# Where a fused attention and expert kernel loads its small constants, and four moves beside it

## The chip, the cores and the metric

One core of a Trainium2 chip. The time is that of the device in microseconds (us), the median of several executions; lower is better.

## The reference

Float32 throughout. Attention over 4 batches, 8 heads, 768 positions, head size 64, with a window and a linear bias:

```python
scores = scale * np.matmul(q, k.transpose(0, 1, 3, 2))
is_global = pos[None, :] < int(n_global)                  # 8
is_local = (rel >= 0) & (rel < int(n_local))              # 96
dist = np.where(is_global & ~is_local, float(n_local), np.abs(rel))
scores = np.where(is_global | is_local, scores - slopes[:, None, None] * dist, -1e9)
a = softmax(scores)
x = np.matmul(a, v)                                       # rows of 512, 3072 tokens
logits = x @ w_gate + modality_bias[modality_id]          # 8 experts
e_idx = np.argmax(logits, axis=1)
out[mask] = gate_w[mask, None] * (np.maximum(x[mask] @ w1[e], 0.0) @ w2[e])
```

Each token goes to one expert and is scaled by that expert's probability.

## The kernel before, in words

The 3072 tokens are 24 blocks of 128 (`NBLK`), six to a batch. The attention half runs as 25 steps (`step(n)`, lines 1257 to 1322) that work on several blocks at a time: step n computes the scores of block n (`s_mm`, line 209, TensorE, eight heads in the order 7, 0, 2, 3, 4, 5, then 1, 6), adds the bias table and finds each row's extreme (`mx`, line 224, VectorE, one instruction per head), takes exponentials (`ex`, line 240, ScalarE), multiplies block n - 2 with the values (`pv`, lines 279 and 290, TensorE, a part with the small tiles `vl` and one with the large tiles `va`), divides by the row sums (`rinv`, `xr`), transposes the exponentials of block n - 1 (`t_mm`, line 254) and copies them out of PSUM as `pT` (`t_cp`: the first and third copy on ScalarE, the second on VectorE, line 261 or 263). The gate of older blocks (`gate_a` to `gate_d`, lines 335 to 360) runs in the same steps, and after the last block of a batch its routing: `route_a`, `route_a2`, `route_e`, `route_b` (counts by two matmuls at lines 411 and 412, a copy to SBUF at line 414, running sums on GpSimd at line 417), `route_d` and `route_c` (scatter of token numbers, line 440). From batches 0 and 1 the first three expert slots are planned in steps 17 and 18 (`plan_0` to `plan_3`, VectorE), and their weights are loaded and split meanwhile (line 657 on GpSimd, lines 646 and 661 on VectorE). The expert half (two layers in split float32, lines 689 to 691 and 731 to 733) follows the steps; the plan of the remaining slots (`items`, `slots`, `granules`) runs beside its first slots, drawn from `rest()` by `fill`.

Three things set the order. On TensorE, ScalarE, VectorE and GpSimd the order of the steps is the order in which the code calls (`manual_schedule`, lines 1237 to 1240); before the steps, and for VectorE and GpSimd in the expert half, a scheduler may move instructions whose inputs are ready (so line 561, a comparison of two constant tiles in `granules`, runs in the first 5 us). Extra work of a step stands in `todo`, `last_work` and `spaced`; `todo[n]` is called after the exponentials of step n and before its transposes, except `route_b` and `route_e`, which wait until the end of the step (`tail_work`). SyncE issues nearly all loads and stores, in its own scheduled order. Completion semaphores are handed out in turn to the transfers of SyncE and ScalarE together, so an issue can stand until the transfer that used its semaphore before has landed.

PSUM: ring `pR` of three banks (scores, one block fills all three: heads 0, 2, 4; heads 1, 3, 5; heads 6, 7), ring `pP` of three (transposes, counts of batches 0 to 2), ring `pX` of two (values).

The start. GpSimd clears the first columns of `kt` (line 124); SyncE loads queries and keys of blocks 0 and 1 (256 and 272 KB a block) and the values of block 0; ScalarE issues the five small loads of `consts_l` (lines 1025 to 1032: gate weights, modality numbers, modality bias and two scalars spread over 128 partitions); TensorE runs 40 warm-up matmuls (line 134). Meanwhile GpSimd and VectorE build a distance tile (lines 145 to 168), from which come two bias tables of eight heads: `tbl0` for the first block of a batch (line 183, ScalarE) and `tbl` for the others (line 185, GpSimd), in the order `HEADS` = 7, 0, 2, 6, 4, 1, 3, 5. The constants are first read in step 3 (`consts_m`, `consts_b`), step 4 (`gate_b`) and step 7 (`consts_d`).

Of the kernel before, what the change touches and what calls it, by code (L numbers as in the profile page):

```python
# [14 lines left out]
ALU = mybir.AluOpType  # L15
# [6 lines left out]
NP = H // 2  # L22
DM = H * D
E = 8
FF = 1024
NT = B * S
NBLK = NT // P
NG0, NL0 = 8, 96
NB = S // P
W = NL0 + NG0 + 64  # L30
C1 = 40
PER = P + NG0
# [4 lines left out]
BE = 2  # L37
# [5 lines left out]
NR = NI - NS  # L43
NGT = 16
# [13 lines left out]
D1 = D + 1  # L58
HEADS = (7, 0, 2, 6, 4, 1, 3, 5)


def bc(ap, n):
    return ap.unsqueeze(2).broadcast_to([ap.shape[0], ap.shape[1], n])


def bm(ap, n):
    return ap.unsqueeze(1).broadcast_to([ap.shape[0], n, ap.shape[1]])
# [3 lines left out]
def moe_attention_kernel(ctx, tc, q, k, v, qs, ks, vr, vo32, n_global, n_local, modality, w_gate, mod_bias, w1, w2, out):  # L71
    nc = tc.nc
# [7 lines left out]
    def p_p(name):  # L80
        return psum.tile([P, 512], F32, tag="pP", name=name, bufs=3)
# [4 lines left out]
    def p_t(name):  # L86
        return psum.tile([P, 512], F32, tag="pR", name=name, bufs=3)
# [33 lines left out]
                vo32[b, i, h].rearrange("p x a d -> p (x a d)"),  # L121
            )

    nc.gpsimd.memset(kt[:, :, 0:PER], 0.0)
    load_kq(0)
    load_kq(1)
    loadv(0)
# [39 lines left out]

    V.tensor_add(mm0, mm0, dd)

    ident = const.tile([P, P], F32, name="ident")  # L170
    make_identity(nc, ident)
    prs = [a1.tile([P, PRW], F32, name=f"pr{i}") for i in range(NPR)]
# [3 lines left out]

    last = [None]

    def table(t, h, m):

        f = -8.0 * 2.0 ** (-(h + 1))
        if t is tbl0:
            last[0] = nc.scalar.mul(t[:, h, :], m, f)
        else:
            nc.gpsimd.tensor_scalar(t[:, h, :], m, f, None, ALU.mult)  # L185


    blk, pss, scs, pts, gt, lgts, rt, xrs = {}, {}, {}, {}, {}, {}, {}, {}
# [79 lines left out]

    pxs = {}

    def pv(n):
        m = n + 2
        r = n % NV
        px = pxs[n] = [p_x(f"x{n}_{h}") for h in range(2)]
        for hp in range(NP):
            for h in range(2):
                hs = slice(64 * h, 64 * h + C1)
                for half in range(2):
                    nc.tensor.matmul(  # L279
                        px[h][64 * half : 64 * half + 64, hp * D1 : (hp + 1) * D1],  # L280
                        pT_of(n, hp, 1)[hs, 64 * half : 64 * half + 64],
                        vl[r][hs, half, hp, :],
                        start=(hp == 0),
                        stop=False,
                        skip_group_check=True,
                    )
        for hp in range(NP):
            for h in range(2):
                for half in range(2):
                    nc.tensor.matmul(  # L290
                        px[h][64 * half : 64 * half + 64, hp * D1 : (hp + 1) * D1],
                        pT_of(n, hp, 2 * h)[:, 64 * half : 64 * half + 64],
                        va[r][:, half, 2 * hp + h, :],
                        start=False,
                        stop=(hp == NP - 1),
                        skip_group_check=True,
                    )
        if n > 2:
            gate_c(*gates(n - 3), px[1])
        if n > 1:  # L300
            if m in pss:
                gate_b(*gates(n - 2), pss.pop(m)[2], 2 * W)
            else:
                gate_b(*gates(n - 2), p_t(f"lp{m}"), 0)
# [89 lines left out]
    def behind(ins, other):  # L394

        if other is not None:
            tc.add_manual_dep(
                ins.ins,
                other.ins.name,
                mybir.DependencyInfo(mybir.DependencyClass.Sync, mybir.DependencyReason.DATA),  # L400
                reason="spaced",
            )

    def route_b(b, pk=None, o=NP * D1 + 32):


        oh = rt.pop(b)
        if pk is None:
            pk, o = p_t(f"pk{b}"), 0
        ohf = oh.rearrange("p a e -> p (a e)")  # L410
        nc.tensor.matmul(pk[:, o : o + NB * E], tri, ohf, start=True, stop=True)
        nc.tensor.matmul(pk[:, o + NB * E : o + 2 * NB * E], ones, ohf, start=True, stop=True)
        pks = gp.tile([P, 2 * NB * E], F32, tag="pks", name=f"pks{b}", bufs=1)
        V.tensor_copy(pks, pk[:, o : o + 2 * NB * E])
        eng = nc.gpsimd if b + 1 < B else V
        for j in range(NB):
            eng.tensor_add(base[:, b, j + 1, :], base[:, b, j, :], pks[:, (NB + j) * E : (NB + j + 1) * E])
        if b + 1 < B:
            eng.tensor_copy(base[:, b + 1, 0, :], base[:, b, NB, :])
        pos = t3(b, "pos")  # L420
        eng.tensor_tensor(pos, pks[:, 0 : NB * E].rearrange("p (a e) -> p a e", e=E), base[:, b, 0:NB, :], ALU.add)
        eng.tensor_tensor(pos, pos, bm(ebase, NB), ALU.add)
        eng.tensor_tensor(pos, pos, oh, ALU.mult)
        rt[b, "pos"] = pos
# [114 lines left out]
    def granules(uex, ust, uli):  # L539

        def pl(name, shape, dt=F32):
            return plan.tile([P] + shape, dt, name=f"g{name}")

        iex, ist, ili = uex[:, NS:NI], ust[:, NS:NI], uli[:, NS:NI]
        nr = pl("nr", [NR])
        V.tensor_sub(nr, ili, ist)
        h1 = pl("h1", [NR])
        V.tensor_scalar(h1, nr, 0.0, None, ALU.is_gt)  # L550
        h2 = pl("h2", [NR])
        V.tensor_scalar(h2, nr, 128.0, None, ALU.is_gt)
        m = pl("m", [1])
        V.reduce_sum(m, h1, axis=AX.X)
        m2 = pl("m2", [1])
        V.reduce_sum(m2, h2, axis=AX.X)
        gi = uidx[:, 0:NGT]
        gm = pl("gm", [NGT])
        V.tensor_scalar(gm, gi, m, None, ALU.subtract)
        s1 = pl("s1", [NGT, NR])  # L560
        V.tensor_tensor(s1, bc(gi, NR), bm(uidx[:, 0:NR], NGT), ALU.is_equal)
        V.tensor_tensor(s1, s1, bm(h1, NGT), ALU.mult)
        s2 = pl("s2", [NGT, NR])
        V.tensor_tensor(s2, bc(gm, NR), bm(uidx[:, 0:NR], NGT), ALU.is_equal)
        V.tensor_tensor(s2, s2, bm(h2, NGT), ALU.mult)
        yield
        gst, gex, gli = pl("st", [NGT]), pl("ex", [NGT]), pl("li", [NGT])
        w = pl("w", [NGT, NR])
        wr = pl("wr", [NGT])
        V.reduce_sum(wr, s2, axis=AX.X)  # L570
        V.tensor_add(s1, s1, s2)
        for dst, src in ((gst, ist), (gex, iex), (gli, ili)):
            V.tensor_tensor(w, s1, bm(src, NGT), ALU.mult)
            V.reduce_sum(dst, w, axis=AX.X)
        V.scalar_tensor_tensor(gst, wr, 128.0, gst, ALU.mult, ALU.add)
        V.tensor_add(m, m, m2)
        V.tensor_sub(m2, gli[:, NGF:NGR], gst[:, NGF:NGR])
        V.tensor_scalar(m2, m2, float(MR), None, ALU.is_gt)
        V.scalar_tensor_tensor(m2, m, float(NGR), m2, ALU.is_gt, ALU.max)
        V.tensor_scalar(m, m, -float(NGF), 0.0, ALU.add, ALU.max)  # L580
        V.tensor_mul(m, m, m2)
        V.tensor_copy(lcnt, m)

        V.tensor_scalar(m, m, 1.0, None, ALU.min)
        V.tensor_copy(m2, flag)
        V.tensor_tensor(m, m, m2, ALU.max)
        V.tensor_copy(past, m)
        yield
        return gex, gst, gli
# [392 lines left out]
    def at(n, f, *args):  # L982
        todo.setdefault(n, []).append((f, args))
# [92 lines left out]
        nc.gpsimd.memset(lto, 0)  # L1076
        nc.gpsimd.memset(ltv, 0.0)

    consts_l()

    nid = (E * NT + U) * IDW // P
    zrow = a2.tile([P, nid // 8], I32, name="zrow")

# [9 lines left out]
    for b in range(B):  # L1093
        n0 = b * NB
        at(n0 + NB + 4, route_a, b)
        at(n0 + NB + 4, route_a2, b)
        at(n0 + NB + 4, route_e, b)
        at(n0 + NB + 4, route_b, b)
        if b != BE:
            at(n0 + NB + 5, route_d, b)  # L1100
        for j in range(NB):
            if b < BE:
                spaced.setdefault(n0 + NB + 5 + (j if j < 4 or not b else j - 1), []).append((b, j))
            else:
                at(max(n0 + NB + 5, NBLK + 1), route_c, b, j)
    at(1, consts_a)
    at(3, consts_m)
    last_work[3] = [(consts_b, ())]
    for j in range(8):
        at(3 + j, consts_c, j)  # L1110
    at(7, consts_d)
    for h in HEADS:
        table(tbl, h, mm)
    load_kq(2)

# [141 lines left out]
    def step(n):  # L1257
# [2 lines left out]
        load(n)  # L1260
        work, mid_work, tail_work = todo.pop(n, []), [], []
        if on:
            s_mm(n, (7, 0, 2, 3, 4, 5))
            mx(n, 7)
            s_mm(n, (1, 6))
            for hh in HEADS[1:]:
                mx(n, hh)
            if n == 1:
                t_mm(0, 0)
                t_cp(0, 0, True)  # L1270
            for hh in HEADS:
                ex(n, hh)
                if hh == 0:
                    mark[0] = last[0]
        if n > 1:
            pv(n - 2)
        if len(spaced.get(n, ())) > 1:
            route_c(*spaced[n].pop(0), mark[0])
# [31 lines left out]
        if n > 2:  # L1310
            gate_a(*gates(n - 3))
        for f, args in tail_work:
            if f is route_b:
                args += (p_p(f"pk{args[0]}"), 0)
            f(*args)
        for f, args in last_work.pop(n, []):
            if f in (split, ld_w):
# [268 lines left out]
```

## Time and profile before

| | us |
|---|---|
| median of 3 executions | 459.52 (456.77 to 464.5) |
| the profiled execution | 453.91 |
| its span, first to last instruction | 452.2 |
| TensorE busy in it | 432.7 |
| VectorE, ScalarE, GpSimd busy | 301.1, 273.9, 109.3 |

The span is what the views below divide; some 1.7 us of the execution lie outside it. The 25 steps of the attention take the first 150 us, 5.44 us for a step in which nothing waits; the experts take the rest. TensorE's busy time hides two things: matmuls overlap and their ends are modelled, and a matmul at the lower clock counts as busy as one at the higher. A wait for several semaphores is put down to the one that came last by the profile; where the engine named had long been done, it was another, often a transfer.

### The profile page before, as it was taken

The numbers are of one execution on the slowest core, as the hardware profiler recorded it, in microseconds if no ns is written. First come the engines' busy times: TensorE is split into PE (matmuls) and PEld (weight loads), VectorE is DVE, ScalarE is ACT, GpSimd is POOL, SyncE is SP. The second block draws the span as 40 slices with busy tenths as digits, with TensorE's granted clock in tenths as the row PEclk, the third lists the DMA queues.
The fourth block names the chain that finished last, engine by engine and source line by source line (L and its number), as shares of the span: only waits on it lengthen the run. The fifth ranks groups of instructions, "written<-read, shape, count | busy, mean of one in ns | idle before, by whom it ended". The sixth has DMA issues, their size and how long they took to land.

```text
span 452.2 us, 12800 instructions
## 1 busy us (share of the span) xinstructions
PE 432.7 (96%) x4873; PEld 382.1 (85%) x4873; DVE 301.1 (67%) x943; ACT 273.9 (61%) x508; POOL 109.3 (24%) x176
## 2 busy tenths in 40 slices
PE   6999999999989999999999999999999999999990
PEld 5889888887978898989898988989889898989850
DVE  4787888788788768987475696574956746464500
ACT  4788888887876455555464576455864645554420
POOL 8010003122415166330504032121123030301010
PEclk9999999999999999999999999999999999999996
DMA  6999999897958749484858489766797666565500
GB/s 187 328 327 347 345 334 310 248 296 237 290 173 313 247 146 378 161 300 156 308 181 287 162 287 335 233 235 213 250 361 260 224 232 215 181 208 208 188 32 28
DMA packets 58666, 110.24 MB, mean 244 GB/s; under 512 B 9019, under 2 KB 22867, under 8 KB 58596
## 3 DMA queue, kind: packets, MB, share of 16 engines
q1 hardware_dynamic: 53312, 96.39, 63.7%
q0 software_dynamic: 4672, 12.85, 7.6%
q8 instruction: 40, 0.66, 0.6%
q14 instruction: 30, 0.25, 0.2%
q10 hardware_dynamic: 612, 0.10, 0.1%
HBM read 94.95 MB, written 14.43 MB: 242 GB/s over the span
## 4 chain that ended last, share of the span: by engine, by line
PE 74%; issue 13%; DVE 4%; POOL 3%; DMA 2%; ACT 1%; POOLq 0%; SPq 0%; ACTq 0%; DVEq 0%
PE s L209 7%; PE pt L254 6%; PE phs L691 5%; PE phs L689 5%; PE phs L690 5%; PE x L290 5%; PE pos L733 4%; PE pos L732 4%; PE pos L731 4%; PE x L279 3%; PE phe L689 3%; PE phe L691 3%; PE phe L690 3%; PE poe L733 2%; PE poe L732 2%
## 5 line engine op out<-in xcount | busy, mean ns | idle before, releaser
L240 ACT ACTIVATE pr<-sc,nmx 128x168 f32<-128x168 f32 x192 | 67.6, 424 | 14.3 <-DVE nmx L224 11.8
L691 PE MATMUL phs<-xhs,als 128*128 128x256 f32 x256 | 72.4, 283 | 0.0
L689 PE MATMUL phs<-xhs,ahs 128*128 128x256 f32 x256 | 72.4, 283 | 0.0
L690 PE MATMUL phs<-xls,ahs 128*128 128x256 f32 x256 | 72.3, 282 | 0.0
L224 DVE CUSTOM_DVE_ANT_0 sc<-s,tbl 128x168 f32<-128x168 f32 x192 | 52.7, 329 | 20.8 <-PE s L209 20.4
L696 DVE SCALAR_TENSOR_TENSOR hls<-phs,hhs 128x512 fp32r<-128x512 f32 x32 | 22.1, 692 | 51.0 <-ACT hhs L695 51.0
L731 PE MATMUL pos<-bhs,hhs 128*128 128x512 f32 x128 | 52.0, 406 | 0.0
L733 PE MATMUL pos<-bhs,hls 128*128 128x512 f32 x128 | 50.7, 396 | 0.0
L732 PE MATMUL pos<-bls,hhs 128*128 128x512 f32 x128 | 50.5, 395 | 0.0
L613 POOL DMA_INDIRECT xgs<-x_rows,uis x16 | 21.1, 1319 | 118.4 <-DMA uis<-ids_sorted 56.5
L689 PEld LDWEIGHTS phs<-xhs,ahs 128*128 128x128 f32 x256 | 49.0, 191 | 0.4
L690 PEld LDWEIGHTS phs<-xls,ahs 128*128 128x128 f32 x256 | 48.9, 191 | 0.3
L691 PEld LDWEIGHTS phs<-xhs,als 128*128 128x128 f32 x256 | 48.9, 191 | 0.0
L695 ACT ACTIVATE hhs<-phs 128x512 fp32r<-128x512 f32 x32 | 19.1, 597 | 49.1 <-PE phs L691 49.1
L209 PE MATMUL s<-kt,qt 64*64 64x168 f32 x768 | 40.8, 329 | 3.8 <-POOL tbl L185 2.5
L209 PEld LDWEIGHTS s<-kt,qt 64*64 64x64 f32 x768 | 31.8, 141 | 9.1 <-DVE nmx L224 2.7
L254 PE MATMUL pt<-ident,pr 128*128 128x128 f32 x288 | 38.0, 283 | 0.0
L254 PEld LDWEIGHTS pt<-ident,pr 128*128 128x128 f32 x288 | 32.2, 144 | 4.8 <-issue 3.4
L440 POOL DMA_INDIRECT ids_sorted<-tki,pi x24 | 25.8, 1074 | 42.3 <-ACT pr L240 28.9
L261 ACT COPY pT<-pt 128x512 f32<-128x512 f32 x49 | 28.3, 585 | 10.0 <-PE pt L254 9.3
L801 POOL DMA_INDIRECT out<-obs,ois x16 | 17.1, 1067 | 54.9 <-ACT obs L800 52.7
L731 PEld LDWEIGHTS pos<-bhs,hhs 128*128 128x128 f32 x128 | 24.1, 189 | 6.6 <-issue 2.1
(348 smaller groups left out, 1000.1 us busy)
## 6 DMA issues: line engine op xcount, KB each, us to landing
va<-in_vr SPq DMA_DIRECT2D x24, 520.0 KB
kt<-in_ks SPq DMA_DIRECT2D x24, 272.0 KB
qt<-in_qs SPq DMA_DIRECT2D x24, 256.0 KB
x_rows<-xr SPq DMA_DIRECT2D x24, 256.0 KB
vl<-in_vo SPq DMA_DIRECT2D x48, 81.2 KB
rawe0a<-in_moe_w SPq DMA_DIRECT2D x4, 512.0 KB
rawe0b<-in_moe_w SPq DMA_DIRECT2D x4, 512.0 KB
rawe1a<-in_moe_w SPq DMA_DIRECT2D x4, 512.0 KB
```

What stands on the lines that cost most here:

```text
L209: nc.tensor.matmul(ps[g][64 * half : 64 * half + 64, c0 : c0 + W], qt[hs, hp, 64 * half : 64 * half + 64], kt[hs, hp, w0 : w0 + W], start= ...
L224: V.tensor_tensor_reduce(out=sc, in0=pss[n][g][:, c0 : c0 + W], in1=(tbl0 if n % NB == 0 else tbl)[:, hh, :], op0=ALU.add, op1=ALU.min, sc ...
L240: last[0] = nc.scalar.activation(pr[:, h * (PRW - W) : h * (PRW - W) + W], scs.pop((n, hh)), AF.Exp, bias=blk[n][:, hh : hh + 1], scale=-1.0,)
L254: nc.tensor.transpose(tp[:, j * P : (j + 1) * P], prs[(NP * n + hp) % NPR][:, o : o + P], ident)
L261: last[0] = nc.scalar.copy(pT.rearrange("p a b -> p (a b)"), tp)
L440: ins = nc.gpsimd.indirect_dma_start(out=ids, out_offset=bass.IndirectOffsetOnAxis(ap=pi[:, j : j + 1], axis=0), in_=tki[:, b * NB + j, :] ...
L689: nc.tensor.matmul(o, hi[:, fs], s.xh[:, c, :], start=(c == 0), stop=False)
L690: nc.tensor.matmul(o, hi[:, fs], s.xl[:, c, :], start=False, stop=False)
L691: nc.tensor.matmul(o, lo[:, fs], s.xh[:, c, :], start=False, stop=(c == 3))
L731: nc.tensor.matmul(s.po[t], s.hh[:, fc, tt], hi[:, wv], start=(fc == 0), stop=False)
L732: nc.tensor.matmul(s.po[t], s.hh[:, fc, tt], lo[:, wv], start=False, stop=False)
L733: nc.tensor.matmul(s.po[t], s.hl[:, fc, tt], hi[:, wv], start=False, stop=(fc == 7))
```

## The change

1. The memset of `kt` is called after the distance chain, not first on GpSimd.
2. `consts_l` is no longer called ahead of the steps but in step 1's `todo`, behind `consts_a`; its five issues stay on ScalarE, now behind step 1's exponentials and ahead of its third `pT` copy.
3. Of the eight `tbl` tables GpSimd computes five (7, 0, 2, 6, 4); VectorE computes the last three (1, 3, 5) in step 0, behind its eight reductions.
4. In steps 17 and 18 the scores of heads 1 and 6 stand between the two parts of the values of block n - 2 (`mid`), and reductions and exponentials go 7, 0, 2, 4, 3, 6, 1, 5. What followed the values' matmuls in `pv` is now `pv_g`, called behind the exponentials as before.
5. `route_b` of batch 2 leaves the end of step 22: its two matmuls (`route_p`) stand behind the first six heads' scores of step 23, the rest behind that step's reductions. The counts of batch 3, in the expert half, take a bank of `pP`, not of `pR`.
6. The comparison of line 561 gets a wait for the ScalarE instruction called last before it, so it can't run in the first microseconds any more.

```diff
-    nc.gpsimd.memset(kt[:, :, 0:PER], 0.0)
     load_kq(0)
...
     V.tensor_add(mm0, mm0, dd)
+    nc.gpsimd.memset(kt[:, :, 0:PER], 0.0)
     ident = const.tile([P, P], F32, name="ident")
...
-    def table(t, h, m):
+    def table(t, h, m, eng=None):
...
-            nc.gpsimd.tensor_scalar(t[:, h, :], m, f, None, ALU.mult)
+            (eng or nc.gpsimd).tensor_scalar(t[:, h, :], m, f, None, ALU.mult)
...
-    def pv(n):
-        m = n + 2
+    def pv(n, mid=None):
...
+        if mid is not None:
+            mid()
         for hp in range(NP):
...
+        if mid is None:
+            pv_g(n)
+
+    def pv_g(n):
+        m = n + 2
+        px = pxs[n]
         if n > 2:
             gate_c(*gates(n - 3), px[1])
...
+    def route_p(b):
+        o = 0
+        pk = rt[b, "pk"] = p_p(f"pk{b}")
+        ohf = rt[b].rearrange("p a e -> p (a e)")
         nc.tensor.matmul(pk[:, o : o + NB * E], tri, ohf, start=True, stop=True)
         nc.tensor.matmul(pk[:, o + NB * E : o + 2 * NB * E], ones, ohf, start=True, stop=True)
+
+    def route_b(b):
+        oh = rt.pop(b)
+        if (b, "pk") not in rt:
+            rt[b] = oh
+            route_p(b)
+            rt.pop(b)
+        pk, o = rt.pop((b, "pk")), 0
         pks = gp.tile([P, 2 * NB * E], F32, tag="pks", name=f"pks{b}", bufs=1)
...
-        V.tensor_tensor(s1, bc(gi, NR), bm(uidx[:, 0:NR], NGT), ALU.is_equal)
+        behind(V.tensor_tensor(s1, bc(gi, NR), bm(uidx[:, 0:NR], NGT), ALU.is_equal), last[0])
...
-    consts_l()
...
-        at(n0 + NB + 4, route_b, b)
+        if b != BE:
+            at(n0 + NB + 4, route_b, b)
...
     at(1, consts_a)
+    at(1, consts_l)
...
-    for h in HEADS:
+    for h in HEADS[0:5]:
         table(tbl, h, mm)
...
+            split_pv = n in (LAST - 1, LAST)
+            heads = (7, 0, 2, 4, 3, 6, 1, 5) if split_pv else HEADS
             s_mm(n, (7, 0, 2, 3, 4, 5))
+            if n == NBLK - 1:
+                route_p(BE)
             mx(n, 7)
-            s_mm(n, (1, 6))
-            for hh in HEADS[1:]:
+            if split_pv:
+                pv(n - 2, lambda: s_mm(n, (1, 6)))
+            else:
+                s_mm(n, (1, 6))
+            for hh in heads[1:]:
                 mx(n, hh)
+            if n == 0:
+                for h in HEADS[5:]:
+                    table(tbl, h, mm, V)
+            if n == NBLK - 1:
+                route_b(BE)
...
-            for hh in HEADS:
+            for hh in heads:
                 ex(n, hh)
...
-        if n > 1:
+        if on and split_pv:
+            pv_g(n - 2)
+        elif n > 1:
             pv(n - 2)
...
         for f, args in tail_work:
-            if f is route_b:
-                args += (p_p(f"pk{args[0]}"), 0)
             f(*args)
```

## Rows read from the trace of the kernel before

**Rows 1.** The page: busy time, share of the span and instructions of each engine.

```profile
PE 432.7 (96%) x4873; PEld 382.1 (85%) x4873; DVE 301.1 (67%) x943; ACT 273.9 (61%) x508; POOL 109.3 (24%) x176
```

**Rows 2.** Waits of PE, whole span: who waited for whom; us in total, times, longest.

```profile
PE s L209 <- POOL tbl L185: 2.5, 1, 2.5
...
PE s L209 <- DVE nmx L224: 1.4, 3, 0.6
...
PE x L290 <- DMA rawe0a<-in_moe_w: 1.3, 1, 1.3
...
PE pk L411 <- ACT pT L261: 0.6, 3, 0.2
```

**Rows 3.** Timeline, first 12.5 us: start, length, engine, line, operation, count, [idle before].

```profile
0.81 0.55 POOL L124 MEMSET kt<- 128x544 f32 x1 [0.29 <-POOLq L1543]
...
0.81 0.41 ACTq L1025 DMA_DIRECT2D wg<-in_wg  x1
...
1.25 0.65 ACTq L1027 DMA_DIRECT2D mi<-in_moe_modality_id  x1
...
1.93 0.37 ACTq L1029 DMA_DIRECT2D mb<-in_moe_modality_bias  x1
...
2.33 0.45 ACTq L1032 DMA_DIRECT2D gi<-in_n_global  x1
...
2.94 0.26 DVE L154 TENSOR_SCALAR mm<-dd 128x168 f32<-128x168 f32 x1
...
3.63 0.34 ACTq L1032 DMA_DIRECT2D gi<-in_n_local  x1
...
4.38 0.29 DVE L561 TENSOR_TENSOR gs<-uidx 128x144 f32<-128x144 f32 x1
...
5.86 5.26 POOL L185 TENSOR_SCALAR tbl<-mm 128x168 f32<-128x168 f32 x8
...
10.10 0.33 DVE L224 CUSTOM_DVE_ANT_0 sc<-s,tbl 128x168 f32<-128x168 f32 x1 [0.80 <-PE s L209]
...
11.68 0.33 DVE L224 CUSTOM_DVE_ANT_0 sc<-s,tbl 128x168 f32<-128x168 f32 x1
```

**Rows 4.** By stretch: us, busy us of PE, PEld, DVE, ACT, POOL, PEclk, DMA share, GB/s.

```profile
4.00:8.00 4.00, 1.53 (x18) 1.29 (x16) 1.85 (x10) 3.25 (x9) 2.98 (x7) 1.00 0.53 147
...
8.00:16.00 8.00, 7.44 (x74) 6.31 (x75) 4.60 (x33) 3.73 (x11) 3.04 (x5) 1.00 0.98 317
```

**Rows 5.** Waits of SP's own queue, 0 to 9 us.

```profile
SPq L119 <- DMA kt<-in_ks: 3.7, 1, 3.7
```

**Rows 6.** Timeline of PE, 7 to 22 us.

```profile
7.98 2.52 PE L209 MATMUL s<-kt,qt 64*64 64x168 f32 x32 [2.47 <-POOL tbl L185]
...
13.95 2.82 PE L254 MATMUL pt<-ident,pr 128*128 128x128 f32 x12
...
20.18 1.53 PE L254 MATMUL pt<-ident,pr 128*128 128x128 f32 x12
...
21.64 1.56 PE L209 MATMUL s<-kt,qt 64*64 64x168 f32 x32
```

**Rows 7.** Timeline of ACT, 15 to 19 us (step 1 and its copy).

```profile
15.10 0.59 ACT L261 COPY pT<-pt 128x512 f32<-128x512 f32 x1 [2.24 <-PE pt L254]
...
15.58 2.71 ACT L240 ACTIVATE pr<-sc,nmx 128x168 f32<-128x168 f32 x8
...
18.20 0.56 ACT L261 COPY pT<-pt 128x512 f32<-128x512 f32 x1
```

**Rows 8.** Timelines of DVE and PE, step 18.

```profile
106.07 0.68 DVE L263 COPY pT<-pt 128x512 f32<-128x512 f32 x1
...
106.67 0.32 DVE L224 CUSTOM_DVE_ANT_0 sc<-s,tbl 128x168 f32<-128x168 f32 x1
...
107.06 0.36 PE L209 MATMUL s<-kt,qt 64*64 64x168 f32 x2 [0.64 <-DVE nmx L224]
```

**Rows 9.** Timeline of DVE, step 24.

```profile
147.28 1.29 DVE L676 TENSOR_TENSOR xle<-mte,xhe 128x512 fp32r<-128x512 f32 x2
```

More of the change, by code (lines that the diff above doesn't have):

```diff
@@ L402, in behind @@
             )
[L404 to L410, printed above, removed]
+    def route_p(b):
+        o = 0
+        pk = rt[b, "pk"] = p_p(f"pk{b}")
+        ohf = rt[b].rearrange("p a e -> p (a e)")
         nc.tensor.matmul(pk[:, o : o + NB * E], tri, ohf, start=True, stop=True)
         nc.tensor.matmul(pk[:, o + NB * E : o + 2 * NB * E], ones, ohf, start=True, stop=True)
+    def route_b(b):
[5 more added lines that the diff above has]
+        pk, o = rt.pop((b, "pk")), 0
         pks = gp.tile([P, 2 * NB * E], F32, tag="pks", name=f"pks{b}", bufs=1)
```

## The prediction, made before the changed kernel was built or timed

> **What bounds the kernel now.** I read the page first: TensorE is busy for 432.7 of 452.2 us [rows 1], so whatever the change does, it can win back part of some 19 us of idle TensorE and no more. I then asked for the waits of TensorE [rows 2], to see where that idle time lies next to the edits. The largest wait is 2.5 us in front of the first scores (line 209). 1.4 us more come from the same line waiting for VectorE's score reductions (line 224) in three places, and 0.6 us from three waits in front of the routing counts (line 411). The 1.3 us at line 290 names a transfer that the change doesn't touch. So the change has some 4 us within its reach, nearly all in the first 20 us, and I read those closely: the timeline of the start [rows 3], transfers by stretch [rows 4], SyncE's queue [rows 5], TensorE and ScalarE in steps 0 and 1 [rows 6, 7].
>
> The view blames table work on GpSimd for the first wait. That can't be it: what the scores need from GpSimd is the memset of kt, over at 1.36 us [rows 3]. SyncE's queue shows the other candidate: the first vl issue waits 3.7 us for a kt load [rows 5], up to about the moment at which the scores start, 7.98 [rows 6]. So the first keys land at about 7.9 us. In that time the transfer engines are only 0.53 busy and move 147 GB/s, against 317 GB/s just after [rows 4]; the five small constant loads are in flight then [rows 3]. And the matmuls run at the lower of TensorE's two levels (1.2 GHz, not 2.4) through steps 0 and 1, judged by their length: twelve transposes take 2.82 us at 13.95 and 1.53 us at 20.18, 32 score matmuls 2.52 us at 7.98 and 1.56 us at 21.64 [rows 6]. The granted-clock column reads 1.00 in both stretches [rows 4], so here I go by the lengths.
>
> **The change part by part.** I sum against the profiled execution: span 452.2 us, 453.9 in all, 5.6 us below the median of the runs, 459.5.
>
> *Constants out of the start, and the memset behind the table chain.* Queries and keys of block 0 are 528 KB; at 317 GB/s [rows 4] they take 1.7 us, and without the constants I expect them to have landed before the warm-up ends at 5.51 (7.98 minus the idle 2.47 [rows 6]). Scores then start at 5.55, 2.4 us sooner. GpSimd's memset moves by 0.55 us behind the iotas and is still long over. The table chain begins 0.55 us sooner and loses the 0.29 us of the granule comparison (line 561) that VectorE runs inside it [rows 3], so the first table is ready for the first reduction.
>
> *Steps 0 and 1.* VectorE's second score reduction starts 2.12 us after the scores (10.10 against 7.98), and the last 1.58 us after that, with 0.33 us of its own [rows 3]. At the low level that gives 5.55 + 2.12 + 1.58 + 0.33 = 9.6 us. The second half of the next block's scores must wait for this bank: 20 of 32 matmuls, 1.6 us, then four transposes, 0.94 us [rows 6]: 12.2 us, where ScalarE's first pT copy started at 15.10 [rows 7], a gain of 2.9. If TensorE, now busy without a break from the warm-up on, has reached the high level by then, the 2.12 shrink to 1.3 (by 1.56 to 2.52 [rows 6]) and the last reduction ends at 8.8. Then VectorE's three tables, 0.26 us each by the nearest row [rows 3], and the next block's first reduction, for which head 6 waits, come last, 9.9 us, and with head 6 and four transposes (0.1 and 0.5) it is 10.5, a gain of 4.6. I take the middle, 3.7. At the low level the tables' 0.8 us end before the scores do and cost nothing; GpSimd is relieved of 2.0 of its 5.26 us [rows 3].
>
> *What ScalarE pays in step 1.* The five issues now stand on ScalarE between the exponentials of step 1 and ScalarE's second pT copy (block 0's third), which follow each other without a gap (15.58 plus 2.71, next at 18.20 [rows 7]). Behind them wait that copy, hence the second half of block 0's values on TensorE, and all of step 2's exponentials. The issues took 0.41, 0.65, 0.37, 0.45 and 0.34 us [rows 3], 2.2 in sum. Bounds: below, nothing, if ScalarE's sequencer issues them while exponentials still run; above, 2.2 plus a wait. The fifth issue stood 0.85 us behind the fourth's end [rows 3], and SyncE once waited 3.7 us [rows 5] for an earlier transfer: an issue can wait for a landing, and from 8 us on the transfer engines are 0.98 busy [rows 4]. I take 2.2 without a wait, nearest to the five rows. Net for the start: 3.7 - 2.2 = 1.5 us, between 4.6 and 2.9 - 5.9 = -3.0. The constants are first read in steps 3 and 4, some 5 us later. SyncE, no longer behind the constants, issues its loads earlier; those had room already.
>
> *Heads 1 and 6 between the values' parts, steps 17 and 18.* In step 18 TensorE waits 0.64 us for the first score reduction (107.06 [rows 8]). The values' first part would fill that, but it needs the pT copy that VectorE runs from 106.07 to 106.75, right in front of the reduction (106.67 to 106.99) [rows 8]. So TensorE restarts some 0.25 us sooner only, and heads 1 and 6 come some 0.6 us later to a VectorE that is behind. I count 0, between +0.6 (the stall gone) and -0.3 (VectorE later, step 19 waits).
>
> *Batch 2's counts after the first scores of step 23.* TensorE no longer stands in front of them: 0.6 us over three places, 0.2 for this one [rows 2]. VectorE's copy and GpSimd's sums come later in the step, and with them a cast whose remainder VectorE takes ahead of line 676, which ends at 148.57 [rows 9] and feeds the first layer; I count +0.2, between 0 and +0.4 with that in the way.
>
> *Last granule counts behind ScalarE.* One comparison of 0.29 us [rows 3] goes into the expert stage, where TensorE has work without a gap; it would cost 0.3 if VectorE had become late there. 0. Batch 3's counts take a buffer of another ring, at no cost for the same reason.
>
> Sum: 1.5 + 0 + 0.2 + 0 = 1.7 us: 452.2 for a profiled execution, 457.8 us against the median.
>
> **The rivals.**
> *The issues wait on ScalarE (slower).* If the five constants are queued behind transfers that land late, ScalarE stands still with the copy and step 2's exponentials behind it. The start's gain, 3.7 in the middle, is used up when the five take over about 3.7 us together; with one wait of 3.7 the start loses 3.0, with the 0.2 of step 23 in all -2.8: 462.3 us. For it: a transfer engine share of 0.98 [rows 4] and the two waits seen. Against: SyncE issues in the same stretch keep up with TensorE.
>
> *Nothing of the issues is seen, and the clock is high early (faster).* 4.6 + 0.2 = 4.8 us: 454.7. For it: TensorE has no break between warm-up and scores. Against: ScalarE had no gap there [rows 7]. The Trainium skill, page Perfetto Trace Analysis, section Sequencer Loop, has a sequencer push engine work into a queue and go on to the next instruction, which would put the issues beside the exponentials; no run here shows it yet.
>
> *The first keys land no sooner (the change doesn't do what it says).* The constants are 98 KB, 0.3 us at 317 GB/s [rows 4]. If bytes alone count, the scores start 0.3 us sooner, and ScalarE still pays 2.2: 0.3 - 2.2 + 0.2 = -1.7, 461.2 us. The Trainium skill, DMA: Bandwidth & Descriptors, section Issuing engines are not separate DMA queues, speaks for it: issuing from several engines saves only the sequencer's time, as all transfers share the same sixteen engines. Against it the trace has these engines half idle, 0.53, just while the small packets are under way [rows 4].
>
> **How the numbers follow.** Forecast 0.47 (457.8 us), waiting issues 0.20 (462.3), everything hidden 0.20 (454.7), keys no sooner 0.13 (461.2). The three runs before spread over 7.7 us (456.8 to 464.5), more than any of these cases, so the range takes the cases and some of that spread: 452 to 463.5 us. About 2% (9 us) is what a measurement of this kernel can tell from no change, and every case lies within it; only the spread reaches beyond: faster 0.04, same 0.93, slower 0.03.
>
> **What would show it.** Right: the first scores start near 5.5 us with no wait in front; the warm-up and line 209 join; the five issues stand on ScalarE's queue after step 1's exponentials, about 2.2 us long, and the second pT copy follows them at about 17 us; step 2's values wait for that copy; step 3 starts 1 to 2 us before 21.64. The wait at line 411 is gone in step 23 and line 561 has left the start. Wrong: a first score start above 7 us; a gap of several us among the five issues; a longer wait of TensorE in step 2 than the 2.5 us won; a new wait in step 19.

## The result: slower, and the profile after

The changed kernel takes 462.6 us (median of 6 executions, 461.12 to 464.06), the kernel before beside it 456.86 us (6 executions): a ratio of 1.0128 [1.0092, 1.0165], slower by 1.3% or 5.7 us. A second comparison, with an experiment below, gave 1.0169 [1.0132, 1.0206]. Both are under the 2% that the prediction took for what can be told from no change, but neither interval takes in 1. The first three of the six executions before are those of the median of 459.52 us named above; one of them, 464.5 us, fell in a slower state of the chip and is left out of the ratio.

The waits of TensorE in the changed kernel's profile (span 460.8 us, 462.75 us in all) come first, as in [rows 2]. The line numbers have shifted: the values' two parts are lines 278 and 291, the counts lines 416 and 417.

```profile
PE x L278 <- ACT pT L261: 9.3, 1, 9.3
PE x L278 <- issue: 1.9, 3, 1.3
...
PE s L209 <- DMA kt<-in_ks: 0.6, 1, 0.6
...
PE pk L416 <- ACT pT L261: 0.4, 2, 0.2
```

The 2.5 us in front of the first scores [rows 2] have become 0.6, and one of the three waits for the counts is gone. In their place stands one wait of 9.3 us for ScalarE's copy. What ScalarE did then is in its timeline (start, length, engine, line, operation, count, idle before), to be set against [rows 7]:

```profile
11.41 0.59 ACT L261 COPY pT<-pt 128x512 f32<-128x512 f32 x1 [1.09 <-PE pt L254]
11.89 2.71 ACT L240 ACTIVATE pr<-sc,nmx 128x168 f32<-128x168 f32 x8
16.55 0.38 ACTq L1039 DMA_DIRECT2D wg<-in_wg  x1
19.46 0.56 ACTq L1041 DMA_DIRECT2D mi<-in_moe_modality_id  x1
20.43 0.36 ACTq L1043 DMA_DIRECT2D mb<-in_moe_modality_bias  x1
21.82 0.33 ACTq L1046 DMA_DIRECT2D gi<-in_n_global  x1
22.57 0.34 ACTq L1046 DMA_DIRECT2D gi<-in_n_local  x1
22.95 0.59 ACT L261 COPY pT<-pt 128x512 f32<-128x512 f32 x1 [8.34 <-DMA mb<-in_moe_modality_bias]
```

In [rows 7] the second copy follows the eight exponentials without a gap; here 8.35 us lie between (14.60 to 22.95). The five issues are 0.33 to 0.56 us long, 1.97 us together. The rest, 6.4 us, is the time in which ScalarE stands in front of them: 1.95, 2.53, 0.41, 1.03 and 0.42 us. Each of these issues carries a wait on the completion semaphore that it takes over. `wg`'s is that of the queries' load issued at 10.50 us, eight transfers earlier in the order in which semaphores are handed out, and the last `gi` waits for `wg` itself. In the trace these earlier transfers land at 16.53, 19.44, 20.40, 21.80 and 22.55 us, and each issue starts 0.02 to 0.03 us later. For `mb` the chain of work shows it (start, length, what): a load of values from its issue to its landing at 20.40, and 0.02 us behind that the start of `mb`.

```profile
13.42 6.99 DMA vl<-in_vo
20.40 0.02 issue
20.43 2.50 DMA mb<-in_moe_modality_bias
```

The transfer engines are full in this stretch or nearly so, as the view by stretch shows (us, busy us of PE, PEld, DVE, ACT, POOL, granted clock, transfer engines' share, GB/s):

```profile
8.00:16.00 8.00, 5.84 (x100) 4.77 (x100) 7.00 (x48) 5.51 (x17) 1.49 (x3) 1.00 1.10 325
16.00:24.00 8.00, 0.42 (x8) 0.30 (x8) 0.00 (x0) 1.05 (x3) 0.00 (x0) 0.55 0.86 270
24.00:32.00 8.00, 8.00 (x153) 7.56 (x150) 5.04 (x29) 6.20 (x18) 0.00 (x0) 0.81 0.73 234
```

From 16 to 24 us nearly the whole core stands, and TensorE's granted clock falls to 0.55 and is still at 0.81 in the next stretch. TensorE's timeline shows what that costs, beside [rows 6]:

```profile
6.06 1.79 PE L209 MATMUL s<-kt,qt 64*64 64x168 f32 x32 [0.55 <-DMA kt<-in_ks]
...
10.72 1.53 PE L254 MATMUL pt<-ident,pr 128*128 128x128 f32 x12
...
23.58 0.49 PE L278 MATMUL x<-vl,pT 40*64 40x65 f32 x8 [9.30 <-ACT pT L261]
24.01 2.00 PE L291 MATMUL x<-va,pT 128*64 128x65 f32 x32
25.94 2.06 PE L254 MATMUL pt<-ident,pr 128*128 128x128 f32 x12
27.93 1.42 PE L209 MATMUL s<-kt,qt 64*64 64x168 f32 x30
```

The twelve transposes take 1.53 us at 10.72, where [rows 6] have 2.82 for the first block's: before the wait TensorE ran at the higher level (2.4 GHz) already. Behind it the same twelve take 2.06 us. Step 3 starts at 27.93 us, in [rows 6] at 21.64: 6.3 us later, though step 2 started 4.5 us sooner (12.18 against 16.70). From step 3 on the two kernels keep this distance within 0.6 us to step 19. So the loss is in the first 28 us. (The two spans differ by more, 8.6 us; the profiled execution of the kernel before is shorter than its median, 453.91 us, and what lies behind step 19 differs between two profiles of one kernel as well, as shown below.)

### The profile page after: what moved, and what is told of

The parts are those of the page before. It is cut to its first block, busy times and chain, and to the rows that moved or that the text cites. A ratio compares the mean times of both kernels' runs of the same rounds, so it can differ in the third digit from the quotient of the medians.

```text
span 460.8 us, 12810 instructions
## 1 busy us (share of the span) xinstructions
PE 434.0 (94%) x4873; PEld 381.1 (83%) x4873; DVE 301.3 (65%) x946; ACT 274.4 (60%) x508; POOL 109.8 (24%) x173
## 4 chain that ended last, share of the span: by engine, by line
PE 72%; issue 13%; DMA 5%; DVE 4%; POOL 2%; ACT 2%; SPq 0%; POOLq 0%; ACTq 0%; DVEq 0%
PE s L209 6%; PE pt L254 6%; PE phs L705 5%; PE x L291 5%; PE phs L703 5%; PE phs L704 5%; PE pos L747 4%; PE pos L746 4%; PE pos L745 4%; PE x L278 3%; PE phe L703 3%; PE phe L704 3%; PE phe L705 3%; PE poe L747 2%; PE poe L745 2%
## 5 line engine op out<-in xcount | busy, mean ns | idle before, releaser
L209 PE MATMUL s<-kt,qt 64*64 64x168 f32 x768 | 39.2, 314 | 1.3 <-DVE nmx L224 0.6
L454 POOL DMA_INDIRECT ids_sorted<-tki,pi x24 | 26.8, 1117 | 42.1 <-ACT pr L240 32.6
L209 PEld LDWEIGHTS s<-kt,qt 64*64 64x64 f32 x768 | 29.8, 133 | 6.3 <-DVE nmx L224 2.0
L278 PE MATMUL x<-vl,pT 40*64 40x65 f32 x768 | 21.5, 223 | 11.6 <-ACT pT L261 9.3
L815 POOL DMA_INDIRECT out<-obs,ois x16 | 17.6, 1098 | 52.7 <-ACT obs L814 50.6
```

What stands on the lines that cost most here:

```text
L209: nc.tensor.matmul(ps[g][64 * half : 64 * half + 64, c0 : c0 + W], qt[hs, hp, 64 * half : 64 * half + 64], kt[hs, hp, w0 : w0 + W], start= ...
L278: nc.tensor.matmul(px[h][64 * half : 64 * half + 64, hp * D1 : (hp + 1) * D1], pT_of(n, hp, 1)[hs, 64 * half : 64 * half + 64], vl[r][hs, ...
```

## The experiments

**Four ways to place the five loads.** Theory A: the loss is ScalarE's wait for the semaphores of earlier transfers, with the lower clock behind it. First, `consts_l` goes back ahead of the steps and all other edits stay:

```diff
+    consts_l()
...
     at(1, consts_a)
-    at(1, consts_l)
```

> The kernel after, with the five constant loads back ahead of the steps; the other five edits stay. Theory A (the five issues on ScalarE in step 1 each stand until an earlier transfer has landed, and everything behind them waits): the 9.3 us wait of TensorE in step 2 is gone, the scores start at 7 to 8 us again, step 3 starts between 20.3 and 21.6 us, and the time is within 1.5 us of the kernel before, rather below it. Rival B (the other edits cost the time, the issues only show in the trace): still 4 us or more above the kernel before.

Second, the opposite: in the kernel before, `consts_l` alone is moved to step 1, and nothing else.

```diff
-    consts_l()
...
     at(1, consts_a)
+    at(1, consts_l)
```

> The kernel before, with nothing changed but the place of the five constant loads (step 1 on ScalarE). Theory A: ScalarE has a gap of 6 to 9 us between step 1's exponentials and the pT copy, TensorE waits about as long in step 2, step 3 starts 5 to 8 us later than 21.64, and the time is 4 to 8 us above the kernel before. Rival B: no such gap, time within 1.5 us of the kernel before.

Third, GpSimd issues the five in step 1, all other edits stay:

```diff
-        nc.scalar.dma_start(wg.rearrange("p c e -> p (c e)"), w_gate)
+        nc.gpsimd.dma_start(wg.rearrange("p c e -> p (c e)"), w_gate)
...
```

> The kernel after, with the five constant loads issued by GpSimd in the same place of step 1, a queue with completion semaphores of its own. Theory A: ScalarE goes from step 1's exponentials to the copy without a gap, the scores start at about 6 us as in the kernel after, step 3 starts near 17.5 to 18.5 us and the time is 2.5 to 5 us below the kernel before. Rival C (the small transfers themselves, in the full queue, hold up the loads that step 2 needs, whoever issues them): step 3 starts after 21.6 and the time is not below the kernel before.

Fourth, they stay on ScalarE in step 1, but behind the copy and not ahead of it:

```diff
-    at(1, consts_l)
+    last_work[1] = [(consts_l, ())]
```

> The kernel after, with the five constant loads still on ScalarE but at the end of step 1, behind block 0's third pT copy. Theory A: the values of block 0 no longer wait, but the gap of ScalarE stays (5 to 9 us), now ahead of step 2's exponentials; TensorE waits in front of step 2's transposes or step 3 instead, step 3 starts 2 to 6 us after 21.64, and the time is 1 to 6 us above the kernel before. Rival D (only that one copy was in a bad place): step 3 starts at 17.5 to 19 us and the time is 2 us or more below the kernel before.

| loads | ratio to before | step 3 starts at, us | ScalarE's gap in steps 1 and 2 |
|---|---|---|---|
| first: at the start, other edits stay | 0.9983 [0.9944, 1.0023] | 20.21 | none |
| second: ScalarE in step 1, nothing else | 1.0213 [1.0152, 1.0275] | 29.27 | 10.11 |
| third: GpSimd in step 1 | 0.9989 [0.9957, 1.0021] | 17.16 | none |
| fourth: ScalarE, behind the copy | 1.0158 [1.0102, 1.0215] | 17.65, step 4 at 32.08 (27.40 before) | 8.50 |

The move of the loads alone makes the loss, and undoing it alone takes the loss away. Behind the copy the same wait only hits the next thing in ScalarE's queue, the exponentials of step 2; TensorE then waits 5.1 us in the middle of step 3 for the reductions behind them. Some sizes that Theory A gave were missed: the second's gap is longer than 9 us and its median 8.8 us above that of the kernel before, where 4 to 8 was expected, and in the fourth not step 3 comes late but what follows inside it. From GpSimd, whose transfers got semaphores of their own (five that no transfer before had used), the issues wait for nothing:

```profile
9.61 0.79 POOL L1039 DMA_DIRECT2D wg<-in_wg  x1
10.42 0.59 POOL L1041 DMA_DIRECT2D mi<-in_moe_modality_id  x1
10.99 0.55 POOL L1043 DMA_DIRECT2D mb<-in_moe_modality_bias  x1
11.53 0.54 POOL L1046 DMA_DIRECT2D gi<-in_n_global  x1
12.06 0.53 POOL L1046 DMA_DIRECT2D gi<-in_n_local  x1
```

The Trainium skill, DMA: Bandwidth & Descriptors, section Anatomy of one DMA — SWDGE (gpsimd) path, says that DMA engines do not wait on semaphores and that any such wait happens on the issuing sequencer. ScalarE's rows agree: the wait stands in its own queue, ahead of its copy.

The time of the third was a miss: step 3 starts 4.5 us sooner than before, the time is only some 0.5 us lower, and the interval takes in a ratio of 1. Runs further on ask where that lead goes.

**One issue alone.** `wg` stays on ScalarE in step 1, the other four go ahead of the steps.

```diff
-    def consts_l():
+    def consts_w():
         nc.scalar.dma_start(wg.rearrange("p c e -> p (c e)"), w_gate)
+
+    def consts_l():
...
+    consts_l()
...
-    at(1, consts_l)
+    at(1, consts_w)
```

> Only the first of the five loads (wg) stays on ScalarE in step 1, the other four go back ahead of the steps. Theory A: the one issue stands until the queries' load issued eight transfers earlier has landed, at 15 to 17 us, some 1 to 3 us behind step 1's exponentials instead of 8.3 us; ScalarE's next copy follows within 1 us of it, step 3 starts at 20 to 23 us (27.93 with all five), and the time is 455 to 459 us, within 2 us of the kernel before. Rival B (each issue costs ScalarE some 1.7 us of its own in this stretch, 8.3 divided by 5, whatever landed): the gap is 1.7 us, and the issue starts right behind the last exponential, within 0.3 us.

Measured: 459.95 us, 0.9997 [0.9960, 1.0033] of the kernel before (459.67 on this chip), step 3 at 19.85. ScalarE's timeline:

```profile
13.68 2.71 ACT L240 ACTIVATE pr<-sc,nmx 128x168 f32<-128x168 f32 x8
16.01 0.33 ACTq L1039 DMA_DIRECT2D wg<-in_wg  x1
16.39 0.59 ACT L261 COPY pT<-pt 128x512 f32<-128x512 f32 x1
```

Neither theory had this quite right. The issue came at 16.01 as Theory A had it, 0.02 us behind the landing that it waited for (a load of values issued at 10.30, not the queries' load expected), but with four loads at the start the exponentials ran until 16.39, so it stood beside them and the copy followed without a gap. Rival B, a cost of 1.7 us for each issue, falls: an issue whose semaphore comes before the work ahead of it has ended costs ScalarE nothing here. The Trainium skill, Perfetto Trace Analysis, section Sequencer Loop, has the sequencer hand work to its engine and go on; this row agrees, and the changed kernel's rows show its limit: an instruction that waits holds everything behind it.

**SyncE issues the five in step 1**, every other edit stays (`nc.sync.dma_start`).

> The five loads issued by SyncE in step 1, every other edit stays. Theory A: they stand in SyncE's queue for earlier landings as they did on ScalarE, but there only loads are behind them, which have room: ScalarE's copy follows step 1's exponentials within 1 us, step 3 starts at 17 to 19 us, no wait of TensorE in steps 2 to 5 is over 1 us, and the time is within 1 us of that with GpSimd's issues (455 to 457 us). Rival D (the loads behind them come late): a wait of TensorE for keys or values of 2 us or more in steps 2 to 5, step 3 or 4 starts some 2 to 6 us later than with GpSimd's issues, and the time is 459 to 463 us.

```profile
14.83 0.35 SPq L1039 DMA_DIRECT2D wg<-in_wg  x1
15.23 0.84 SPq L1041 DMA_DIRECT2D mi<-in_moe_modality_id  x1
16.11 0.35 SPq L1043 DMA_DIRECT2D mb<-in_moe_modality_bias  x1
16.51 0.43 SPq L1046 DMA_DIRECT2D gi<-in_n_global  x1
17.08 1.45 SPq L1046 DMA_DIRECT2D gi<-in_n_local  x1
```

457.12 us against 459.67, a ratio of 0.9940 [0.9907, 0.9974]; step 3 at 17.62, no wait of TensorE over 0.8 us in steps 2 to 5. The issues come some 5 us later than GpSimd's did: they stand behind SyncE's earlier loads, and the first and the last of them start 0.02 us after a landing that they wait for (14.81 and 17.06). But behind them stand only loads with room. Run again beside GpSimd's on one chip:

> The constants by SyncE in step 1, once more, beside GpSimd's on the same chip: the first gave 0.9940 [0.9907, 0.9974] of the kernel before and the second 0.9989 [0.9957, 1.0021], measured on different chips. Theory A (on either queue ScalarE is free, so the two are the same kernel to TensorE): both lie at 0.991 to 0.998 and within 0.4% of each other. Rival E (GpSimd's issues cost something that SyncE's don't): this one stays at 0.994 or below and GpSimd's at 0.998 or above again.

> The constants by GpSimd in step 1, once more, beside SyncE's on the same chip. Theory A: within 0.4% of SyncE's, 0.991 to 0.998 of the kernel before. Rival E: 0.998 or above, and over 0.4% above SyncE's.

0.9937 [0.9907, 0.9967] by SyncE (449.92 us against 453.16) and 0.9959 [0.9933, 0.9986] by GpSimd, as Theory A had it; the second half of Rival E, 0.998 or above for GpSimd, did not come. SyncE's has the lowest ratio measured, though its interval overlaps that of GpSimd's: it is below the kernel before on two chips, where the changed kernel is above it in both of its comparisons.

**Start edits alone, with GpSimd's issues.** The split in steps 17 and 18 and the move of batch 2's counts are taken back (`split_pv = False`; `route_b` at the end of step 22 again). And the kernel before was profiled once more.

> Theory A (the five issues on ScalarE wait for the landing of earlier transfers whose completion semaphores they take over; nothing else of the change costs more than 0.7 us): with the constants issued by GpSimd in step 1 and the two late edits (heads 1 and 6 in steps 17 and 18, batch 2's counts) taken back, step 3 starts at 17 to 18.5 us as with GpSimd's issues before, steps 17 to 19 take 17.7 to 18.4 us together (18.4 to 18.5 with the split), and step 22 takes 5.8 to 6.0 us (5.43 with the counts moved). In all 2.5 to 4.5 us below the kernel before, 453 to 455. Rival C (the lead won at the start is lost again before the end, in stalls and waits that come wherever the engines run ahead): the time is within 1.5 us of the kernel before, as with GpSimd's issues and all other edits, although step 3 starts 4 us sooner.

> The kernel before, profiled once more, to see how far one profiled execution differs from another in the later stages. Theory A: step 3 starts at 20.5 to 22.5 us again; steps 4 to 16 take 5.2 to 6.2 us each as before; where a stall of 1 to 2 us without a late releaser sits (step 22 in the first profile) differs, so that the stages behind step 16 differ by up to 3 us between the two profiles of the same kernel. Rival C: the later stages agree within 0.5 us, and the differences of 1 to 2.5 us that the changed kernels show behind step 16 are theirs.

The first: 458.87 us against 459.67, 0.9967 [0.9928, 1.0005], step 3 at 17.12. That is 1.5 us below before, not 2.5 to 4.5, and the interval takes in a ratio of 1; so with or without the late edits the time gains less than step 3 does. One place where the lead shrinks is step 12. TensorE's timeline of the kernel with SyncE's issues, in its first run:

```profile
70.90 1.53 PE L254 MATMUL pt<-ident,pr 128*128 128x128 f32 x12
74.02 0.66 PE L342 MATMUL tx<-ident,xr 128*128 128x128 f32 x4 [1.59 <-ACT pT L261]
```

and the same step in its second run:

```profile
70.38 1.53 PE L254 MATMUL pt<-ident,pr 128*128 128x128 f32 x12
71.76 0.66 PE L342 MATMUL tx<-ident,xr 128*128 128x128 f32 x4
```

One kernel, two executions, and step 12 took 7.17 and 5.44 us. This stall of 1.6 to 1.9 us also stood in the profiles of GpSimd's issues (first run), of the start edits alone and of the second experiment, not in either profile of the kernel before. But that kernel loses time in the next step instead: its step 13 takes 5.99 and 6.63 us, that of SyncE's issues 5.72. Over both steps the loss on the chip that profiled both is 0.8 us (12.89 against 12.07). The row at 74.02 blames ScalarE, but ScalarE's own next instruction was waiting for TensorE. The cause of the stall stays open. The second profile of the kernel before (459.51 us) starts step 3 at 21.08 and agrees with the first in steps 3 to 12 within 0.01 us each, yet reaches the first layer of the later expert slots 4.2 us later than the first profile (226.78 against 222.62), more than either expectation had (up to 3 us, and 0.5). So what happens behind step 16 can't be told from one profile of each kernel. It seems to go by the chip more than by the kernel: from the first layer to the first layer of the later slots it takes 73.14 us in the first profile of the kernel before and in all five profiles of the two chips on which that kernel's median is about 453 us, and 73.6 to 77.2 us in the other nine.

The late edits themselves can be read from the steps' lengths, on the chip that ran both forms (from the first row of line 209 in one step to that in the next):

| us | before again | start edits alone | one issue (late edits in) | SyncE (late edits in) |
|---|---|---|---|---|
| step 17 | 6.04 | 6.03 | 5.62 | 5.61 |
| step 18 | 6.93 | 6.96 | 6.54 | 6.51 |
| step 19 | 5.44 | 5.44 | 6.38 | 6.40 |
| sum of 17 to 19 | 18.41 | 18.43 | 18.54 | 18.52 |
| step 22 | 5.86 | 5.86 | 6.46 | 5.90 |

On this chip the split wins 0.4 us in each of steps 17 and 18 and gives 0.9 back in step 19. On the two chips of about 453 us the five profiles with the split have 17.21 to 17.42 for the three steps together; none without it was taken there, and the first profile of the kernel before, which resembles them behind step 16, has 17.74. So the split may win 0.3 us there, which no run on one chip shows. Step 22 without the counts takes 5.44 in three profiles (the changed kernel, both times, and the fourth experiment), 0.4 less than 5.86; in the other eight it takes 5.73 to 6.88.

**The clock behind the wait.** 150 matmuls whose product nobody reads are put on TensorE in the changed kernel just ahead of the eight that wait; first beside a kernel before of 453.16 us, and then once more beside the changed kernel itself.

```diff
         for hp in range(NP):
+            if n == 0 and hp == NP - 1:
+                fill = p_p("fill")
+                for i in range(150):
+                    nc.tensor.matmul(fill[:, 0:P], warm, warm, start=True, stop=True)
             for h in range(2):
```

> The changed kernel with 150 matmuls more, whose product nobody reads: warm by warm, put on TensorE in step 2 just ahead of the eight matmuls of line 278 that wait 9.3 us for ScalarE's copy. ScalarE's issues wait as before. Theory A (the idle TensorE falls to the lower level and pays for it after the wait): the fill takes 7 to 10 us, the granted clock stays at 1.00 to past 27 us, the 32 matmuls of line 291 behind it take 1.15 us and not 2.00, the 12 transposes 1.53 and not 2.06, step 3 starts at 26.2 to 27.0 us (27.93 without the fill), and the time is 1 to 2 us below the changed kernel, 460.5 to 461.6 us where that had 462.6. Rival F (the level falls for another reason, or the records mislead): lengths of 2.0 us again, step 3 at 27.5 us or later, no gain.

> The changed kernel once more, beside the one with the fill on one chip. Theory A: 1.009 to 1.017 of the kernel before as in the first comparison, step 3 at 26.5 to 28.5 us, the granted clock at the lower level for some 10 us from the middle of the wait on.

> The changed kernel with the fill of 150 matmuls once more. The trace of its first run put step 3 at 25.40 us against 27.93, and behind ScalarE's copy 3.46 us against 4.98. Theory A (idle costs 1.5 us behind the wait by the lower level, and nothing else differs): 1 to 2 us below the changed kernel on the same chip, a ratio of 1.005 to 1.014. Rival G (the 1.0192 [1.0134, 1.025] of its first run is its own: the fill costs later what it wins, or the next executions fall lower): at or above the changed kernel's time on the same chip.

TensorE's timeline of the first run with the fill:

```profile
13.46 8.55 PE L278 MATMUL fill<-warm 128*128 128x128 bf16 x150
22.58 0.34 PE L282 MATMUL x<-vl,pT 40*64 40x65 f32 x8 [0.58 <-ACT pT L261]
22.86 1.15 PE L295 MATMUL x<-va,pT 128*64 128x65 f32 x32
23.94 1.53 PE L254 MATMUL pt<-ident,pr 128*128 128x128 f32 x12
25.40 1.56 PE L209 MATMUL s<-kt,qt 64*64 64x168 f32 x32
```

By stretch, its granted clock stays at 1.00 where the changed kernel had 0.55:

```profile
16.00:24.00 8.00, 7.42 (x149) 7.11 (x147) 0.06 (x1) 2.06 (x6) 0.00 (x0) 1.00 0.88 267
```

The matmuls behind the wait have their full speed again, 1.15 and 1.53 us. From ScalarE's late copy to step 3 it takes 3.46 us with the fill, in both runs, as with GpSimd's issues (3.44), and 4.98 and 5.75 without it in the two profiles of the changed kernel (in the second, step 3 starts at 28.56 and the granted clock is still at 0.63 from 24 to 32 us, lower for longer than expected). So the idle TensorE loses its higher level and pays 1.5 to 2.3 us for it. In the whole time this gain doesn't show: 1.0192 [1.0134, 1.0250] in the first run, and side by side 1.0167 [1.0115, 1.0219] with the fill against 1.0169 [1.0132, 1.0206] without. On the time Rival G had it. In the profiled execution of the second run ScalarE's copy came at 24.07, 1.26 us later than in the changed kernel beside it, and steps 8 and 14 were 1.1 and 0.7 us longer; whether the fill causes these is open. Part of the gain is lost by the fill itself: in both runs with it, step 16 takes 6.65 and 6.55 us where both profiles of the changed kernel have 5.86, as TensorE there waits for VectorE's copy (here in the first run) and not, 0.2 us long, for ScalarE's:

```profile
PE pk L420 <- DVE pT L263: 1.0, 1, 1.0
```

The fill takes one bank out of ring `pP`, from which the counts of step 16 come too, so they get another bank than before. And from the last matmul's end to the end of the span it takes 11.29 us in both runs with the fill, 10.83 in both without. Together this is some 1.2 of the 1.5 to 2.3 us won; a fill with a bank of its own was not tried.

## Why the prediction was wrong

**What failed: "What ScalarE pays in step 1".** It took 2.2 us without a wait, between nothing and 5.9. It was 8.35. Two readings failed there. The five lengths in [rows 3] were taken as the price of an issue; but four of those five issues waited for nothing, and the fifth showed the real question, which semaphore an issue takes over. And the upper bound counted one wait of the size seen in [rows 5] for five issues that each have their own: together they waited 6.4 us. The 0.98 share of the transfer engines [rows 4] spoke for such waits and was put aside for the fact that SyncE's issues kept up; but SyncE has nothing behind them that TensorE needs at once.

**What was left out: the clock behind a wait.** The sum had no term for TensorE falling to the lower level in a wait that the change itself makes. It is 1.54 us in the profile of the changed kernel.

**What was right: the gain of the start.** It was put at 3.7 us, 4.6 with the higher clock early. The runs that free ScalarE start step 3 at 17.1 to 17.6, 4.0 to 4.5 us ahead of 21.64 (3.5 to 4.0 ahead of the 21.08 of the second profile before), with the higher level early, as the second rival has it. At ScalarE's first copy, by which the prediction counted, the gain is 3.7 us in the changed kernel (11.41 against 15.10 [rows 7]) and 4.5 with GpSimd's issues (10.63). That the middle of two cases was met in the changed kernel is luck: its scores start at 6.06, not 5.55, and the high level is there early. The first keys land sooner: scores start at 5.1 to 5.7 us in the experiments without small loads at the start (6.06 in the changed kernel's first profile, with 0.55 us of wait for keys), and at 6.9 to 8.0 where all or most of them stand there. With that the rival by which only bytes count is refuted. In the changed kernel 3.6 us of this gain reached ScalarE, so step 3 adds up: 21.64 - 3.6 + 8.35 + 1.54 = 27.93.

**The reading of the low clock by lengths [rows 6] was right.** In the second profile of the kernel before, the granted clock itself shows it; in the first, the record of the clock begins only at 17.23 us.

```profile
0.00:8.00 8.00, 4.88 (x64) 4.74 (x68) 3.81 (x20) 3.35 (x10) 6.65 (x34) 0.96 0.53 152
8.00:16.00 8.00, 7.03 (x94) 5.70 (x90) 5.28 (x34) 5.16 (x15) 2.69 (x5) 0.61 0.92 284
```

**Steps 17 and 18: right on the chip that ran both forms.** Forecast 0; measured there 0.1 us the wrong way, with the give-back in step 19 that the lower end named. In the changed kernel's step 18 TensorE waits 0.16 and 0.27 us for VectorE in two places,

```profile
112.40 0.67 PE L278 MATMUL x<-vl,pT 40*64 40x65 f32 x8 [0.16 <-DVE xr L328]
113.33 0.58 PE L278 MATMUL x<-vl,pT 40*64 40x65 f32 x24 [0.27 <-DVE pT L263]
```

where the kernel before has one wait of 0.64 [rows 8].

**Batch 2's counts: not settled.** 0.2 was taken; step 22 is 0.4 us shorter in three profiles of eleven, and how much VectorE and GpSimd give back ahead of the first layer can't be separated, as that stretch (step 23's start to the first layer) differs by 1.2 us between the two profiles of the kernel before.

**Line 561: right.** The comparison ran in the expert half, and nobody waited for it:

```profile
L575 DVE TENSOR_TENSOR gs<-uidx x1: 303/303/303, 201.0 to 201.0; 128x144 f32<-128x144 f32 x1
```

**The rival that came.** "The issues wait on ScalarE" gave 462.3 us, and 462.6 was measured. Its mechanism is the one that the runs show, and the number was met with two errors that cancel. It set a cost of 5.9 us against a gain of 2.9; the profile has 9.9 (8.35 and 1.54) against 3.6, a loss of 6.3 and not 3.0 at step 3. And it was counted from the median before of 459.5 us, of three executions; all six have 456.9.

## What to carry to other kernels

Before an issue is put into the queue of a computing engine, look up which semaphore it takes over and when the transfer that has it will land: in a stretch with full transfer engines this is the price, for each issue anew, and everything behind it pays. The length of an issue says nothing about it, as one whose semaphore has come ran here beside the exponentials at no cost. If small loads must leave the start, give them to the queue that has nothing but loads behind it, which here won 0.6% over the kernel before where ScalarE lost 1.3%, and add the clock's fall to the price of a long wait of TensorE (1.5 to 2.3 us behind waits of 9.3 and 9.5 us here).

## What the runs showed beyond that

- A lead won in the first 20 us came out smaller in the time: 4.0 and 4.5 us at step 3 with SyncE's issues (against 21.64) became 2.6 and 3.2 us. On the chip that profiled both kernels it is 3.5 us at step 3 (against 21.08), 2.6 at the experts' first layer and 2.0 at the end of the span. But the second run of SyncE's issues lies 5.8 us ahead of the first profile of the kernel before at that layer, so not every profile loses the lead. The stall in step 12 came in one execution of a kernel and not in another.
- GpSimd's issues cost something at the other end: from the last matmul's end to the end of the span it takes 11.8 us with them (both runs with all other edits) and 10.8 us with SyncE's and in the changed kernel (both runs of each); the two profiles of the kernel before have 11.29 and 11.45. The medians of SyncE's and GpSimd's differ by 1.1 us (449.92 and 451.01), with overlapping intervals; why the end is longer was not tried.
- One chip differs from another by more than this change: the kernel before had medians from 452.8 to 459.7 us on the chips used, so a ratio on the same chip is the only comparison that holds.
